# A two-layer FNet and MLP kernel: sums of the next tile, weights' steps and stores at other places in the order

## The chip, the cores and the metric

The kernel runs on one core of a Trainium2 chip. The metric is the device time of one execution in microseconds (us); three runs of the kernel before gave 2624.6, 2624.86 and 2625.03, a median of 2624.86 us. All times below are us unless ns is written. PE is the matrix engine (TensorE), PEld its weight loads, DVE the vector engine, ACT the scalar engine, POOL the GpSimd engine, and SP the queue that issues most transfers.

## The reference

```python
def _A_ref(x, dft_seq_re, dft_seq_im, dft_hid_re, dft_hid_im):
    a = jnp.einsum("bsd,ed->bse", x, dft_hid_re)
    b = jnp.einsum("bsd,ed->bse", x, dft_hid_im)
    y = jnp.einsum("ts,bse->bte", dft_seq_re, a) - jnp.einsum("ts,bse->bte", dft_seq_im, b)
    return y

def _B_ref(x, w1, b1, w2, b2):
    y = _layernorm(x, axis=-1)
    h = _gelu(jnp.einsum("bsd,df->bsf", y, w1) + b1)
    return jnp.einsum("bsf,fd->bsd", h, w2) + b2

x = A_x                                   # 1 x 2048 x 576, float32
x = x + _A_ref(_layernorm(x), ...)        # w1 is 576 x 4608, w2 is 4608 x 576
x = x + _B_ref(_layernorm(x), ...)
x = x + _A_ref(_layernorm(x), ...)
x = x + _B_ref(_layernorm(x), ...)
```

## The kernel before

All matrix products are made in a 2x2 block form with seven products in place of eight, and each float32 operand is cut into a high part (rounded to PE's float32r type by ACT, a "high") and a low part (source minus high, by DVE, a "low"). A product is then three passes: high by high, high by low, low by high (`PASSES`, L47).

**Sequence stage** (class `Sequence`, `run` at L758). The transform along the sequence comes first. Tiles 0 and 1 are made by `first_mms`; then 14 tiles (2 to 15) follow, each of seven products in the order 1, 6, 2, 5, 7, 3, 4 (`ORDER`, L34), each product 24 matmuls of 128x288. For a tile `cs` delivers four blocks of 128x1024 floats (0 to 3), loaded through SP into a ring of six buffers. A buffer that is given back is loaded at once with the next block in the order 0, 2, 3, 1 of the tiles (`load_c`, L677). The operands of products 5, 6, 2 and 7 are sums of blocks, made by DVE: `sums` (L688) makes block 2 + block 3 into a buffer `tmp` and subtracts block 0 from block 2; `low` (L700) goes on with the rest. Product n's low is recorded two products ahead, its high three ahead:

```python
                if n and n + 2 < len(steps):
                    self.low(*steps[n + 2])
                if n % 7 == 2 and t + 1 < NT:
                    self.sums(t + 1)
                self.load_c()
                if n + 3 < len(steps):
                    self.high(*steps[n + 3])
                self.mms(t, i)
```

The engines execute in the order that this code records. The third block of the next tile (block 3) can be loaded only when block 0 of this tile has been given back, which `low` of product 2 does (L705 to L707).

**Weights' steps** (generator `weights`, L264; `pump`, L322). While the first Sequence stage and the first MLP half run, w1 is cut into parts in DRAM, 126 parts in all: loads of 128x384 (`in_w`), GpSimd sums of them, two ACT operations (L284, L285), one DVE low (128x384, shown as 128x3x128) and a store to `w_parts` (L299). One `pump` does either the low of a part and the high of the next, or the store; the two alternate. In the Sequence stage each product but the third of a tile is followed by two pumps (L793 to L795), and there the stores are issued by ACT's queue. In the second layer no parts are left to make.

**MLP** (`mlp`, L1121; `inner`, `outer`). For one half of the rows, w1's products run in 18 steps q of seven products each (`inner`, 49 matmuls of 128x512), w2's in 9 groups g of two q each (`outer`, 128x288). q = 0 is made in two halves of 256 columns, the second inside group 0. Each product, and each half of an outer product, is followed by `advance` (L1195), which counts places: 0 to 6 for the first q of a group, 7 to 14 for the first outer products, 15 to 21 for the second q and so on (in group 0, which has no outer products, 0 to 6 and 7 to 13). At a place it pumps as often as `BEHIND` lists the place, in groups 1 and up; and in the first MLP it makes w2's parts (`make`, L1162): for each of seven products an ACT high (L1169), a DVE low (128x576), GpSimd differences, and a store. In this half the stores go through SP, as do w1's parts on their way back (`R<-w_parts`, by `load_w` at L1144). Group 0's w2 parts are made so: product 1 at places 3 and 4 of group 0; products 5, 6, 3, 7, 4 and 2 in group 1, from place 0 on (L1386 to L1392).

Of the kernel before, what the change touches and what calls it, by code (L numbers as in the profile page):

```python
# [15 lines left out]
P = 128  # L16
NT = S // P
DH = D // 2
NP = NT // 2
NQ = F // P // 2  # L20
NG = NQ // 2
# [40 lines left out]
EXTRA_AT = 7424  # L62
EARLY_X = (12800, 9344, 8192)
EARLY_T = 10496
BEHIND = (0, 2, 2, 4, 5, 6, 15, 16, 16, 17, 17, 19, 21, 21)
H_AT = (8704, 22400)
C2_AT = (OWN_AT, 37760)
Y_AT = (RN - Y_N, 0)
# [92 lines left out]
def spectral_mixer(ctx: ExitStack, tc: tile.TileContext, x, dh, c0, cs, w1, b1, w2, b2, out):  # L161
# [168 lines left out]
    class Sequence:  # L330
# [354 lines left out]
        def block(self, t, k):  # L685
            return self.live[t, k](NP, P)

        def sums(self, t):  # L688
            add(nc.vector, self.tmp(NP, P), self.block(t, 2), self.block(t, 3))
            sub(nc.vector, self.block(t, 2), self.block(t, 2), self.block(t, 0))  # L690

        def source(self, t, i):
            return self.tmp(NP, P) if i == 5 else self.block(t, {1: 0, 6: 0, 2: 1, 7: 2, 3: 1, 4: 3}[i])
# [64 lines left out]
        def run(self, hidden):  # L758
            for p in range(NP):
                while self.ready <= p:  # L760
                    next(self.pieces)
                self.first_mms(p)

            outs = [next(b for b in self.xs if b.at != raw.at)]
            self.xs.remove(outs[0])
            self.first_post(0, outs[0])
            for _ in self.pieces:
                pass
            outs.append(A.place(UV_AT + 4 * D, 2 * D) if outs[0].at < UV_AT + 4 * D else A.place(UV_AT + 6 * D, 2 * D))
            steps = self.steps  # L770
            for n, (t, i) in enumerate(steps):
                self.load_c()
                if n and n + 2 < len(steps):
                    self.low(*steps[n + 2])
                if n % 7 == 2 and t + 1 < NT:
                    self.sums(t + 1)
                self.load_c()
                if n + 3 < len(steps):
                    self.high(*steps[n + 3])
                self.mms(t, i)  # L780
                if n == 1:
                    self.first_turn(0, outs[0])
                    hidden.reserve()
                self.post(t, i)
                if n == 1:
                    self.first_post(1, outs[1])
                if n == 3:
                    self.first_turn(1, outs[1])
                if t == NT - 1:
                    hidden.begin(self, ORDER.index(i))  # L790
                if n == 3 and not self.early:
                    dma(b1t, b1)
                if n % 7 != 2 and n > 3 and (t < NT - 1 or n % 7 < 4):  # L793
                    pump()
                    pump()  # L795
            for k in range(2):
                self.L[k].free()
            self.own.close()
            for z in self.Z:
                z.free()  # L800
            hidden.take()
# [319 lines left out]
    def mlp(hid, store, first, ends, before, after):  # L1121
# [72 lines left out]

        def advance(to=None):  # L1195
            at[1] += to is None
            for _ in range(BEHIND.count(at[0]) if to is None and group[0] else 0):
                pump()
            while kept and kept[0][0] <= at[1]:
                kept.pop(0)[1]()  # L1200
            while due and due[0][0] <= (at[0] if to is None else to):
                due.pop(0)[1]()
            at[0] += 1
# [176 lines left out]
        for k in range(4 * first):  # L1380
            load_raw(0, k)
        for g in range(NG + 1):
            at[0], group[0] = 0, g or not first
            if first and not g:
                soon, late = make(0)
                due.extend((n, step) for n, (_, step) in zip((3, 4), soon))  # L1386
            elif first:
                due.extend(late)
                if g < NG:
                    soon, late = make(g)  # L1390
                    due.extend(soon)
            if g == NG:  # L1392
                work(99)
                hs.close()
            if half == 0 and len(c2.idle) < 4:
                more = R.place(0, 4 * DH)
                if more:
                    c2.idle.append(more)
            for f in range(2):
                if g < NG:  # L1400
                    for _ in inner(2 * g + f, None if g or f else 1):
                        pass
                if g == last and f:
                    c1.close()
                    Y.free()
                    if half == 0 or ends:
                        c2.idle += [R.place(C1_AT[half] + k * 4 * DH, 4 * DH) for k in range(2 + half)]
                    if half == 0:
                        c2.idle += [R.place(UT_AT[1][1] + k * 4 * DH, 4 * DH) for k in range(2)]
                if g == NG:  # L1410
                    if f == 0:
                        advance(6)
                        at[0], slot[0] = 7, 0
                        for k, i in enumerate(LAST):
                            outer(last, i, k % 2)
                elif g:
                    advance(6 + 15 * f)
                    at[0] = 7 + 15 * f
                    slot[0] = 0
                    for i in OUTER[f]:  # L1420
                        outer(g - 1, i, 1 - f)
# [87 lines left out]
```

## Time and profile before

| what | value |
|---|---|
| median of 3 runs | 2624.86 |
| the profiled execution | 2624.75 |
| its span, first to last instruction | 2623.0 |
| PE busy, PEld busy | 2614.4, 2466.3 |
| DVE, ACT, POOL busy | 1836.8, 1120.2, 791.5 |
| PE's granted clock over the span | 1.000 |
| chain that ended last: PE, DVE, transfers | 92%, 5%, 1% |

PE's matmuls are pipelined and their ends are modelled, so a PE that is busy all the time can still start its matmuls later than it could. A stretch that holds a known number of matmuls shows that by its length. The first Sequence stage runs to about 376 us, the first MLP half from about 438 to 870.

### The profile page before, as it was taken

Reading aid. Unit: us, or ns where it says so; the run is one execution under the profiler, and the core shown is the slowest. Engines: PE = TensorE matmul, PEld = TensorE weight load, DVE = VectorE, ACT = ScalarE, POOL = GpSimd, SP = SyncE. Lnnn points to the kernel's source line nnn. Section 1 sums busy time; section 2 is a strip of 40 time slices with the busy share of each in tenths; the row PEclk is TensorE's granted clock in tenths of the full one; section 3 lists DMA queues with packets and bytes.
Section 4 is the critical chain, followed back from the end, with each engine's and each line's share of the span. In section 5 each row is a group of like instructions: output and inputs, shape, how many; then the busy total and the mean of one; then the engine's idle time right before and its main releaser. Section 6 shows DMA issues by size and latency. Waiting matters only on the chain.

```text
span 2623.0 us, 44794 instructions
## 1 busy us (share of the span) xinstructions
PE 2614.4 (100%) x17252; PEld 2466.3 (94%) x17252; DVE 1836.8 (70%) x2580; ACT 1120.2 (43%) x1821; POOL 791.5 (30%) x638
## 2 busy tenths in 40 slices
PE   9999999999999999999999999999999999999999
PEld 9999999899999989998999999999999999899998
DVE  8999987778787765556687776576555557655555
ACT  7555555555553443333354333353333325433332
POOL 5334333544444332222251000132122233322222
PEclk9999999999999999999999999999999999999999
DMA  6667676778788666676544343756666685666664
GB/s 226 223 236 234 234 255 215 266 278 301 279 299 300 178 202 195 194 222 210 173 175 135 122 124 124 211 159 194 193 195 194 195 268 169 199 195 195 194 194 155
DMA packets 223238, 544.91 MB, mean 208 GB/s; under 512 B 23712, under 2 KB 74912, under 8 KB 222880
## 3 DMA queue, kind: packets, MB, share of 16 engines
q1 hardware_dynamic: 210496, 513.91, 62.2%
q10 hardware_dynamic: 12528, 28.12, 2.8%
q8 instruction: 137, 2.24, 0.3%
q14 instruction: 77, 0.63, 0.1%
HBM read 429.87 MB, written 114.72 MB: 208 GB/s over the span
## 4 chain that ended last, share of the span: by engine, by line
PE 92%; DVE 5%; DMA 1%; issue 1%; POOL 1%; ACT 0%; DVEq 0%; ACTq 0%; SPq 0%; POOLq 0%
PE bank L211 91%; DVE R L201 3%; DVE A L201 1%; DMA w_parts<-R 1%; DMA A<-in_cs 0%; PE bank L991 0%; DVE A L198 0%; PE bank L1035 0%; DVE moments L242 0%; PE bank L994 0%; ACT R L698 0%; DMA A<-in_w 0%; DMA R<-w_parts 0%; PE bank L1045 0%; POOL A L198 0%
## 5 line engine op out<-in xcount | busy, mean ns | idle before, releaser
L211 PE MATMUL bank<-R 128*128 128x288 f32 (+2 forms) x16972 | 2585.9, 314 | 3.9 <-DVE R L201 1.2
L211 PEld LDWEIGHTS bank<-R 128*128 128x128 f32 x16972 | 2434.8, 189 | 150.8 <-DVE R L201 4.3
L198 DVE TENSOR_TENSOR A<-bank,A 128x576 f32<-128x576 f32 (+3 forms) x812 | 567.6, 707 | 510.2 <-PE bank L211 457.7
L201 POOL TENSOR_TENSOR R<-A,R 128x512 fp32r<-128x512 f32 (+1 forms) x292 | 380.0, 1310 | 912.4 <-ACT R L1299 560.6
L201 DVE TENSOR_TENSOR R<-A,R 128x1024 fp32r<-128x1024 f32 (+10 forms) x534 | 535.0, 1028 | 34.6 <-ACT R L698 14.3
L1299 ACT ACTIVATE R<-A 128x512 fp32r<-128x512 f32 x288 | 177.5, 630 | 356.4 <-DVE A L201 219.5
L198 POOL TENSOR_TENSOR A<-A 128x576 f32<-128x576 f32 (+2 forms) x102 | 155.0, 1527 | 531.1 <-ACT A L743 338.9
L1234 ACT ACTIVATE bank<-bank,b1t 128x512 f32<-128x512 f32 (+1 forms) x224 | 144.9, 647 | 350.5 <-DVE bank L198 233.6
L698 ACT ACTIVATE R<-A 128x1024 fp32r<-128x1024 f32 x196 | 205.6, 1054 | 123.8 <-PE bank L211 61.0
L198 DVE TENSOR_TENSOR bank<-bank,A 128x512 f32<-128x512 f32 (+1 forms) x228 | 152.3, 670 | 147.7 <-PE bank L211 147.0
L201 POOL TENSOR_TENSOR A<-A 128x288 f32<-128x288 f32 (+3 forms) x152 | 190.3, 1255 | 198.1 <-DVE R L201 103.6
L201 DVE TENSOR_TENSOR A<-A 128x1024 f32<-128x1024 f32 (+3 forms) x166 | 163.5, 989 | 6.2
L201 DVE TENSOR_TENSOR R<-bank,R 128x512 fp32r<-128x512 f32 x232 | 156.1, 676 | 5.5 <-ACT R L1299 5.0
L1299 ACT ACTIVATE R<-bank 128x512 fp32r<-128x512 f32 x216 | 121.0, 595 | 33.9 <-PE bank L211 33.9
L201 DVE TENSOR_TENSOR A<-bank,A 128x512 f32<-128x512 f32 x144 | 98.1, 681 | 0.4
L1261 ACT ACTIVATE A<-bank 128x512 f32<-128x512 f32 (+1 forms) x76 | 43.7, 575 | 120.2 <-PE bank L211 120.1
L284 ACT ACTIVATE R<-A 128x256 fp32r<-128x256 f32 x126 | 51.9, 412 | 63.7 <-DMA w_parts<-R 27.1
L1234 ACT ACTIVATE A<-bank,b1t 128x512 f32<-128x512 f32 (+1 forms) x76 | 50.5, 665 | 63.4 <-DVE bank L198 63.4
L232 POOL TENSOR_TENSOR moments<-moments,power 128x1 f32<-128x1 f32 x32 | 25.5, 797 | 134.9 <-DVE moments L234 117.5
L285 ACT ACTIVATE R<-A,power,middle 128x128 fp32r<-128x128 f32 x126 | 60.6, 481 | 0.0
L258 ACT ACTIVATE A<-A,moments 128x576 f32<-128x576 f32 x58 | 49.3, 867 | 23.7 <-DMA A<-x_mid 11.7
L198 DVE TENSOR_TENSOR A<-A 128x1024 f32<-128x1024 f32 x28 | 35.8, 1277 | 20.0 <-DMA A<-in_cs 12.3
(70 smaller groups left out, 612.9 us busy)
## 6 DMA issues: line engine op xcount, KB each, us to landing
R<-w_parts SPq DMA_DIRECT2D x504, 320.0 KB, 3.4
R<-w_parts SPq DMA_DIRECT2D x189, 576.0 KB, 3.7
A<-in_cs SPq DMA_DIRECT2D x112, 512.0 KB, 4.5
w_parts<-R SPq DMA_DIRECT2D x63, 576.0 KB, 6.2
w_parts<-R ACTq DMA_DIRECT2D x75, 320.0 KB, 4.3
w_parts<-R SPq DMA_DIRECT2D x51, 320.0 KB, 4.9
uv_mid<-A SPq DMA_DIRECT2D x28, 576.0 KB, 5.4
A<-in_w SPq DMA_DIRECT2D x72, 192.0 KB, 5.4
```

What stands on the lines that cost most here:

```text
L198: engine.tensor_tensor(dst, a, b, op=op)
L201: engine.tensor_tensor(dst, a, b, op=OP.subtract)
L211: nc.tensor.matmul(o, a, b, start=start, stop=stop, skip_group_check=True)
L232: nc.gpsimd.tensor_tensor(mv[:, 3:4], mv[:, 2:3], power[:, 0:1], op=OP.pow)
L258: nc.scalar.activation(dst, src, AF.Identity, bias=mv[:, 4:5], scale=mv[:, 3:4])
L284: nc.scalar.activation(t[:, 1:4:2], src[:, 0:3:2], AF.Copy)
L285: nc.scalar.activation(t[:, 2], src[:, 1], AF.Identity, bias=power[:, 2:3], scale=middle)
L698: nc.scalar.activation(self.cells[t, i](2, NP, P)[:, 0], self.source(t, i), AF.Copy)
L1234: nc.scalar.activation(dst, src, AF.Gelu_apprx_tanh, bias=bias(f))
L1261: nc.scalar.activation(up, o, AF.Copy)
L1299: nc.scalar.activation(H[q, k](2, TC)[:, 0], src, AF.Copy)
```

## The change

Five things are moved; no arithmetic is added or taken away.

1. `sums` of the next tile is cut in two: the addition behind the low that is recorded with product 4 of the tile (`n % 7 == 3`), the subtraction with product 5 (`n % 7 == 4`). Before, both stood with the third product.
2. The weights' steps in the Sequence stage are left out behind the seventh product of a tile and no longer behind the third; in the last tile they follow the first five products and no longer the first, second and fourth; in the first tile two products instead of three.
3. `BEHIND` has the same 14 pumps at other places, so that every store stands at a later place than its low.
4. In the second group of the first MLP half a shorter list, `BEHIND_1`, has 12 pumps.
5. w2's parts of products 5 and 6 for group 0 are made at places 5, 6, 12 and 13 of group 0, not at places 0 to 3 of group 1.

```diff
-BEHIND = (0, 2, 2, 4, 5, 6, 15, 16, 16, 17, 17, 19, 21, 21)
+BEHIND = (0, 2, 4, 4, 6, 6, 15, 16, 17, 17, 19, 19, 21, 21)
+BEHIND_1 = (0, 2, 4, 4, 15, 16, 17, 17, 19, 19, 21, 21)
...
-        def sums(self, t):
-            add(nc.vector, self.tmp(NP, P), self.block(t, 2), self.block(t, 3))
-            sub(nc.vector, self.block(t, 2), self.block(t, 2), self.block(t, 0))
+        def sums(self, t, which=(0, 1)):
+            if 0 in which:
+                add(nc.vector, self.tmp(NP, P), self.block(t, 2), self.block(t, 3))
+            if 1 in which:
+                sub(nc.vector, self.block(t, 2), self.block(t, 2), self.block(t, 0))
...
-                if n % 7 == 2 and t + 1 < NT:
-                    self.sums(t + 1)
+                if n % 7 in (3, 4) and t + 1 < NT:
+                    self.sums(t + 1, (n % 7 - 3,))
...
-                if n % 7 != 2 and n > 3 and (t < NT - 1 or n % 7 < 4):
+                if n % 7 != 6 and n > 3 and (t < NT - 1 or n % 7 < 5):
                     pump()
                     pump()
...
-            for _ in range(BEHIND.count(at[0]) if to is None and group[0] else 0):
+            for _ in range((BEHIND if group[0] > 1 else BEHIND_1).count(at[0]) if to is None and group[0] else 0):
                 pump()
...
-            at[0], group[0] = 0, g or not first
+            at[0], group[0] = 0, g if first else NG
             if first and not g:
                 soon, late = make(0)
-                due.extend((n, step) for n, (_, step) in zip((3, 4), soon))
+                due.extend((n, step) for n, (_, step) in zip((3, 4, 5, 6, 12, 13), soon + late[:4]))
+                late = late[4:]
```

The built programs show where the instructions went. Lines of the change are numbered one to four higher.

**DVE, one tile of the first Sequence stage, before.** The stretch begins with the row that reads block 0 for the last time (after it block 3 of the next tile can be loaded). `R<-A,R 128x1024` is a low of a product, `128x3x128` a weights' step, `A<-bank` the reading of product 6's sum; the two `A<-A 128x1024` in the middle are the next tile's sums.

```order
L201 TENSOR_TENSOR A<-A 128x1024
L201 TENSOR_TENSOR R<-A,R 128x3x128
L201 TENSOR_TENSOR R<-A,R 128x1024
L198 TENSOR_TENSOR A<-bank,A 128x288
L201 TENSOR_TENSOR R<-A,R 128x3x128
L201 TENSOR_TENSOR R<-A,R 128x1024
L198 TENSOR_TENSOR A<-A 128x1024
L201 TENSOR_TENSOR A<-A 128x1024
L201 TENSOR_TENSOR R<-A,R 128x1024
L201 TENSOR_TENSOR R<-A,R 128x3x128
L201 TENSOR_TENSOR R<-A,R 128x1024
```

The same stretch of the change, from the same row.

```order
L202 TENSOR_TENSOR A<-A 128x1024
L202 TENSOR_TENSOR R<-A,R 128x3x128
L202 TENSOR_TENSOR R<-A,R 128x1024
L199 TENSOR_TENSOR A<-bank,A 128x288
L202 TENSOR_TENSOR R<-A,R 128x3x128
L202 TENSOR_TENSOR R<-A,R 128x1024
L202 TENSOR_TENSOR R<-A,R 128x3x128
L202 TENSOR_TENSOR R<-A,R 128x1024
L199 TENSOR_TENSOR A<-A 128x1024
L202 TENSOR_TENSOR R<-A,R 128x3x128
L202 TENSOR_TENSOR R<-A,R 128x1024
L202 TENSOR_TENSOR A<-A 128x1024
```

The addition (L199) now has a weights' step and a low more between itself and the first row, the subtraction a further two.

**ACT, group 0 of the first MLP half, before.** `R<-A 128x2x288` is the high of a w2 part, `bank<-bank,b1t` and `A<-bank,b1t` are gelus, `A<-bank 128x512` is the copy of product 1's sum of q = 1.

```order
L1169 ACTIVATE R<-A 128x2x288
L1234 ACTIVATE bank<-bank,b1t 128x256
L1234 ACTIVATE A<-bank,b1t 128x256
L1234 ACTIVATE bank<-bank,b1t 128x512
L1299 ACTIVATE R<-bank 128x512
L1261 ACTIVATE A<-bank 128x512
```

The same stretch of the change.

```order
L1172 ACTIVATE R<-A 128x2x288
L1237 ACTIVATE bank<-bank,b1t 128x256
L1172 ACTIVATE R<-A 128x2x288
L1237 ACTIVATE A<-bank,b1t 128x256
L1237 ACTIVATE bank<-bank,b1t 128x512
L1302 ACTIVATE R<-bank 128x512
L1264 ACTIVATE A<-bank 128x512
```

The high of w2's part 5 stands ahead of two gelus and of the copy.

**SP, the second q of group 1, before.** `R<-w_parts 128x640` loads a part of w1, `L299` stores one.

```order
L299 DMA w_parts<-R 128x640
L195 DMA R<-w_parts 128x640
L299 DMA w_parts<-R 128x640
L195 DMA A<-in_w 128x384
L195 DMA R<-w_parts 128x640
```

The same stretch of the change.

```order
L300 DMA w_parts<-R 128x640
L196 DMA R<-w_parts 128x640 x2
L300 DMA w_parts<-R 128x640
L196 DMA A<-in_w 128x384
L196 DMA R<-w_parts 128x640
```

The second load no longer stands behind the second store.

## Rows read from the trace of the kernel before

**Rows 1.** Windows, tiles 5 to 8, 10 and 12 to 15 of the first Sequence; columns in its head line.
```profile
core 0: us, PE busy (x) PEld busy (x) DVE busy (x) ACT busy (x) POOL busy (x), PEclk, DMA share, GB/s
...
126.87:149.27 22.40, 22.40 (x170) 22.28 (x169) 20.89 (x22) 12.69 (x23) 7.63 (x5) 1.00 0.69 240
149.27:172.67 23.40, 22.81 (x170) 22.35 (x169) 21.75 (x22) 12.88 (x23) 6.58 (x5) 1.00 0.66 229
172.67:195.68 23.01, 22.93 (x171) 22.41 (x170) 22.05 (x24) 13.35 (x24) 6.78 (x5) 1.00 0.68 228
195.68:219.07 23.39, 22.73 (x171) 22.35 (x169) 20.49 (x22) 12.80 (x24) 8.02 (x6) 1.00 0.68 232
...
241.34:263.56 22.22, 22.22 (x171) 22.22 (x169) 21.71 (x21) 12.59 (x24) 10.22 (x6) 1.00 0.74 244
...
285.77:308.44 22.67, 22.52 (x171) 22.28 (x169) 21.41 (x22) 12.66 (x23) 7.44 (x5) 1.00 0.68 239
308.44:331.34 22.90, 22.76 (x170) 22.31 (x169) 21.75 (x24) 13.04 (x24) 7.03 (x5) 1.00 0.67 235
331.34:353.91 22.57, 22.52 (x170) 22.28 (x169) 21.68 (x22) 12.49 (x23) 9.18 (x7) 1.00 0.65 222
353.91:376.12 22.21, 22.21 (x170) 22.21 (x169) 18.92 (x24) 16.80 (x29) 6.69 (x5) 1.00 0.80 266
```
**Rows 2.** Groups by form, DVE, 126.87 to 353.91 (tiles 5 to 14): busy, mean ns, idle before.
```profile
L201 DVE TENSOR_TENSOR R<-A,R 128x1024 fp32r<-128x1024 f32 x70 | 98.9, 1413 | 2.7 <-ACT R L698 2.7
L201 DVE TENSOR_TENSOR R<-A,R 128x384 fp32r<-128x384 f32 x60 | 45.0, 750 | 0.0
...
L198 DVE TENSOR_TENSOR A<-A 128x1024 f32<-128x1024 f32 x10 | 13.0, 1304 | 7.9 <-DVE R L201 3.7 <-issue 3.2 <-DMA A<-in_cs 1.0
```
**Rows 3.** Timeline of SP, tile 8: start, duration.
```profile
203.12 0.33 SPq L195 DMA_DIRECT2D A<-in_cs  x1
```
**Rows 4.** Timeline of DVE, tile 8: start, duration, in brackets the idle time before.
```profile
209.18 1.23 DVE L198 TENSOR_TENSOR A<-A 128x1024 f32<-128x1024 f32 x1 [2.08 <-issue]
```
**Rows 5.** Timeline of DVE, lows of product 6 in tiles 10 and 11.
```profile
241.90 1.23 DVE L201 TENSOR_TENSOR R<-A,R 128x1024 fp32r<-128x1024 f32 x1 [0.29 <-ACT R L698]
...
264.41 1.23 DVE L201 TENSOR_TENSOR R<-A,R 128x1024 fp32r<-128x1024 f32 x1 [0.29 <-ACT R L698]
```
**Rows 6.** Groups by form, POOL, 126.87 to 353.91.
```profile
L201 POOL TENSOR_TENSOR A<-A 128x384 f32<-128x384 f32 x25 | 40.0, 1601 | 28.0 <-issue 20.2 <-DMA w_parts<-R 5.8 <-DVE R L201 1.1
```
**Rows 7.** Windows, groups 0 and 1 of the first MLP half.
```profile
452.02:469.77 17.75, 17.75 (x79) 14.53 (x78) 11.14 (x19) 11.46 (x22) 7.67 (x6) 1.00 0.83 271
469.77:501.68 31.91, 30.00 (x168) 25.76 (x166) 26.33 (x39) 17.84 (x36) 17.71 (x14) 1.00 0.68 233
```
**Rows 8.** Timeline of PEld, 440 to 506.
```profile
471.69 1.48 PEld L211 LDWEIGHTS bank<-R 128*128 128x128 f32 x7 [0.57 <-DVE A L198]
474.16 5.54 PEld L211 LDWEIGHTS bank<-R 128*128 128x128 f32 x36 [0.99 <-DVE bank L198]
480.74 18.41 PEld L211 LDWEIGHTS bank<-R 128*128 128x128 f32 x109 [1.04 <-POOL R L201]
499.95 6.20 PEld L211 LDWEIGHTS bank<-R 128*128 128x128 f32 x41 [0.80 <-DVE R L201]
```
**Rows 9.** Timeline of DVE, group 1, low of w2's part 6.
```profile
471.55 0.74 DVE L201 TENSOR_TENSOR R<-A,R 128x576 fp32r<-128x576 f32 x1
```
**Rows 10.** Timeline of SP, second q of group 1.
```profile
495.38 0.32 SPq L299 DMA_DIRECT2D w_parts<-R  x1
```
**Rows 11.** Chain of waits, 440 to 506: start, duration, what.
```profile
496.28 3.57 DMA R<-w_parts
```
**Rows 12.** Timeline of POOL, group 0, both differences for w2's part 1.
```profile
451.76 2.93 POOL L201 TENSOR_TENSOR A<-A 128x576 f32<-128x576 f32 x2 [3.74 <-DVE R L201]
```
**Rows 13.** Timeline of ACT, group 0.
```profile
452.01 0.48 ACT L1234 ACTIVATE A<-bank,b1t 128x256 f32<-128x256 f32 x1 [0.49 <-DVE bank L198]
...
453.84 0.60 ACT L1261 ACTIVATE A<-bank 128x512 f32<-128x512 f32 x1
```
**Rows 14.** Windows, second layer's Sequence.
```profile
1400.00:1500.00 100.00, 100.00 (x759) 100.00 (x758) 69.96 (x68) 39.52 (x51) 9.50 (x10) 1.00 0.41 133
```

## The prediction

> **What bounds the kernel now.** I read the windows view by tile first, then the groups of one engine, then its timeline. PE is busy throughout, but its ends are modelled, so I compare the length of a stretch with the matmuls in it. A Sequence tile is seven products of 24 matmuls. Tile 10 takes 22.22 and tile 15 takes 22.21 [rows 1], that is 22.21 / 168 = 0.1322 a matmul, with weight loads without a gap. I take that as the floor. Above it lie tile 5 by 0.19, tile 6 by 1.19, tile 7 by 0.80, tile 8 by 1.18, tile 12 by 0.46, tile 13 by 0.69 and tile 14 by 0.36 [rows 1]: 4.87 us in all. That is everything the Sequence part of the change can win. In the second layer 759 matmuls in 100 us are again 0.1318 each, with no gap in the weight loads, so nothing is to be had there [rows 14].
>
> What makes these tiles late is DVE. It is busy 20.5 to 22.1 in each, of 22.21 that PE needs [rows 1]. Among its groups only the first of the next tile's sums waits noticeably: 7.9 us before ten of them [rows 2], in part under the name of a transfer, in part as "issue" or as DVE itself. The timeline shows what it is: block 3 of the next tile is issued at 203.12 [rows 3], and the addition starts at 209.18 after 2.08 of waiting [rows 4], 6.06 after the issue. The lows behind it in DVE's order wait too, and PE waits for them.
>
> The second place is the start of the MLP. From 452.02 to 469.77 PE makes 11 products of 7 matmuls (the count of 79 takes in both neighbours), 17.75 / 77 = 0.2305 each [rows 7]. The next stretch, to 501.68, holds ten more such products and 96 outer matmuls: 70 x 0.2305 + 96 x 0.1322 = 28.8, but takes 31.91 [rows 7], 3.1 too long. The weight loads stand still four times there: 0.57 and 0.99 behind DVE, 1.04 behind POOL and 0.80 before 499.95 [rows 8], in all 3.40. Before the last one a load of w1's parts issued at 496.28 lands after 3.57 [rows 11], so that one is a transfer's, though the row names DVE.
>
> **The sums.** Between the last reading of block 0 and the addition stood two weights' steps and two lows, 2 x 0.75 + 2 x 1.41 = 4.3. Now there are three of each, 6.5 [rows 2], against the 6.06 that the load took in the longest wait [rows 3, 4]. I take the waits as gone. DVE then has, in the seven late tiles, a mean of 21.4 us of work (the mean of their DVE column [rows 1]) and room of 0.8 a tile. Nothing else moves against PE: counted from one low of product 6 to the next, DVE does the same work. The lows of products 2, 5 and 7 come a weights' step earlier, those of 3 and 4 by two sums and one sum, those of 1 and 6 unchanged.
>
> Not every tile has room. From the low of product 6 in tile 10 to that in tile 11 are 264.41 - 241.90 = 22.51, without a wait for the load [rows 5], 0.30 more than PE needs. It is covered by a lead: that low ends at 243.13, and product 6 is due at 241.34 + 22.21 / 7 = 244.51, so 1.38 ahead [rows 1, 5]. Tiles with and without room alternate in runs of three or four, because the weights come in sevens and a tile holds six steps; three such tiles use 0.9 of the lead. I leave 0.4 us for what remains and take **4.5 saved**, of bounds 0 and 4.87.
>
> **The weights' steps in the Sequence.** They are as many, but one fewer in tile 2 and two more in tile 15. Tile 15 has DVE busy 18.92 of 22.21 [rows 1]; two steps of 0.75 fit. If that cover were gone (the first hidden products wait for a cut that stands behind them), the cost is at most these 1.5. Taken as 0. The second layer's Sequence has no weights' steps and DVE at 70 of 100 [rows 14]: 0.
>
> **w2's parts 5 and 6 in group 0.** From the stretch 466 to 475 two lows of 0.74 [rows 9], two highs on ACT and one weights' step of 0.75 on DVE [rows 2] go away: 2.2 us of DVE, against stalls of 0.57 + 0.99 behind it [rows 8]. POOL loses one difference of 1.47, half of 2.93 [rows 12], in front of the lows that PE waits 1.04 for [rows 8]. So the first three stalls should go.
>
> What is new stands in group 0. The high of part 5 reads the difference that POOL makes at 451.76, the first of two in 2.93 [rows 12], so it can start only at 453.2. It lasts about 0.7 (the low of that tile takes 0.74 [rows 9]) and stands on ACT ahead of the gelu that started at 452.01 and of the copy at 453.84 [rows 13]. Gelu to copy took 1.83, so the copy starts at 453.2 + 0.7 + 1.83 = 455.8 at the latest and ends at 456.4. The third product of q = 1 writes the bank that is copied and is due at 452.02 + 14 x 0.2305 = 455.25. **A new stall of 0.7 to 1.1; I take 0.95.** Part 6, two places before the end of group 0, has free time on all engines: 0.
>
> **The stores one place later.** In the second q of group 1 the store at 495.38 [rows 10] stands behind a low of its own place, and the load PE waits for can be issued only behind it, at 496.28 [rows 11]. With the load ahead of the store, it can go when its buffer comes free, some 3 us sooner: the last stall, 0.80 by the weight loads, goes. In the other groups of this half I see no stall to win. Together the MLP gives 3.1 - 0.95 = **2.1 saved**, of bounds 2.7 (3.40 - 0.7) and a loss of 1.1 (all stalls stay).
>
> **Sum.** 2624.75 - 4.5 - 2.1 = 2618.15 for the profiled execution. The median of the runs lies 0.11 above it, so 2618.3.
>
> **The rivals.** Two tenths of a per cent, 5.25 us, is about what a measurement of this kernel can tell from no change; below 2619.6 it is faster.
>
> *Contention fills the gap.* DVE's steps are stretched where POOL works: the 1024-wide low takes 1.41 in the mean and 1.23 by itself [rows 2, 5]. If every tile comes to need the 22.51 of tile 10, thirteen tiles lose 0.30 each less the lead of 1.38, so 2.5: only 2.4 are won, 2620.4. For it: waiting tiles have less DVE work than tile 10, as if the wait kept the engines apart. Against it: tile 10 has also the most POOL work, 10.22, and that is given by the weights' order [rows 1].
>
> *A full stop at each meeting.* If DVE, at one more meeting per tile, had to wait out a POOL sum whole, 1.60 [rows 6], the room of 0.8 would leave 0.8 lost in each of thirteen tiles, 10.4 in place of 4.87; with 2.1 won, 2628.3. Against it: 25 such sums last 40.0 in tiles 5 to 14 [rows 6], yet all 70 lows together are stretched by only 70 x 0.18 = 12.6 [rows 2, 5]. The Trainium skill (SBUF — State Buffer, section Who interferes with whom) does say that a DVE instruction with two SBUF inputs and a GpSimd one that reads SBUF exclude each other for a whole instruction; this trace agrees that they hinder each other and not that it is for so long.
>
> *The MLP gives nothing.* The stall behind the new high remains and the others shrink by no more than it costs, because they have a second cause behind the first (the four lows on POOL follow each other with or without the difference). 2624.86 - 4.5 = 2620.4.
>
> *Slower: the load comes later too.* Block 3 is issued through SP in order, behind loads of weights that wait for POOL to free their buffer. If it came so late that the addition still waits 1.5 a tile, DVE would need 21.4 + 0.4 + 1.5 = 23.3, and thirteen tiles would lose 1.1 each, 14: with 4.87 no longer lost and 2.1 won, 2632. It decides from a wait of about 0.8 a tile upward, today's mean. Against it: the change takes away the pumps just ahead of that load, and the largest delay seen is 6.06.
>
> **How the numbers follow.** The forecast has 0.60, contention 0.16, the full stop 0.02, the MLP without gain 0.14, the late load 0.05, no effect at all 0.03. The forecast's own range is 2617.0 to 2620.0 (all of 4.87 and 2.5, or 3.5 and 1.3). The range of 2616.9 to 2622.5 adds both rivals at 2620.4, with 2 us for both at once. Five in six of the forecast and a third of the first two rivals lie below 2619.6: faster 0.61. Above 2630.1 lie the late load and a little of the unknown: slower 0.06. The rest, 0.33, is the same.
>
> **What would show it.** Tiles 5 to 14 at 22.2 to 22.3 each, and no idle time on DVE before its first sums. If the waits are gone and tiles are still long, contention was right; if the addition still waits, the late load. In the MLP: one gap of about 1 us in the weight loads near 455 (moved by what the Sequence saves), with ACT's part-5 high waiting for POOL ahead of it; none of the four later ones. A gap of 2 us there, or the POOL stall still present, would make the MLP's term wrong.

## The result and the profile after

The change is slower, by a quarter of a per cent: a median of 2631.52 us over ten runs (2628.47 to 2635.53) against 2624.89 for ten runs of the kernel before (2623.43 to 2625.95), a ratio of 1.0026 with an interval of 1.0016 to 1.0035. The prediction was 2618.3, in a range that ended at 2622.5. The profiled execution of the change has a span of 2629.1, that of before 2623.0.

To split the 6.1 us I use one mark that every trace has: the short run of weight loads with which the transpositions ahead of the first MLP half end. In the timeline of PEld, before:

```profile
442.61 0.85 PEld L1035 LDWEIGHTS bank<-ident,A 128*128 128x128 f32 x8 [0.17 <-DVE A L201]
```

The same timeline after the change, 440 to 770 (start, duration, line, tiles, count, and in brackets the idle time before with what ended it):

```profile
442.14 0.85 PEld L1038 LDWEIGHTS bank<-ident,A 128*128 128x128 f32 x8 [0.17 <-DVE A L202]
455.41 11.14 PEld L212 LDWEIGHTS bank<-R 128*128 128x128 f32 x49 [0.90 <-ACT A L1264]
468.56 38.65 PEld L212 LDWEIGHTS bank<-R 128*128 128x128 f32 x228 [2.01 <-ACT A L1264]
508.12 45.18 PEld L212 LDWEIGHTS bank<-R 128*128 128x128 f32 x266 [0.91 <-ACT R L1302]
554.61 45.01 PEld L212 LDWEIGHTS bank<-R 128*128 128x128 f32 x266 [1.31 <-ACT R L1302]
600.73 45.02 PEld L212 LDWEIGHTS bank<-R 128*128 128x128 f32 x266 [1.11 <-ACT R L1302]
647.01 44.93 PEld L212 LDWEIGHTS bank<-R 128*128 128x128 f32 x266 [1.27 <-ACT R L1302]
692.78 44.91 PEld L212 LDWEIGHTS bank<-R 128*128 128x128 f32 x266 [0.84 <-ACT R L1302]
738.40 31.69 PEld L212 LDWEIGHTS bank<-R 128*128 128x128 f32 x189 [0.70 <-ACT R L1302]
```

Up to the mark the change wins 0.5 us where 4.5 were forecast; behind it, it loses 6.6 where 2.1 were to be won. The four gaps of [rows 8] are gone. In their place stand two in group 0, of 0.90 and 2.01, and one at the start of every later stretch of outer products, six of them here, 6.14 in all. New less old is 6.14 + 2.91 - 3.40 = 5.65; the other 0.9 lies in pieces too small to name.

**The gap that comes back in every group** is read from the chain of waits of the change, 500 to 560 (start, duration, what):

```profile
498.90 5.17 DMA w_parts<-R
...
543.98 6.58 DMA w_parts<-R
...
550.64 0.18 ACT R L285
...
551.99 1.00 ACT R L1302 x2
...
554.64 5.50 PE bank L212 x33
```

and from ACT's timeline, in group 0 (first two rows) and later:

```profile
452.76 0.69 ACT L1172 ACTIVATE R<-A 128x576 fp32r<-128x576 f32 x1 [1.71 <-POOL A L202]
...
467.91 0.60 ACT L1264 ACTIVATE A<-bank 128x512 f32<-128x512 f32 x1 [4.16 <-POOL R L202]
...
550.64 0.42 ACT L285 ACTIVATE R<-A 128x256 fp32r<-128x256 f32 x1 [3.65 <-DMA w_parts<-R]
```

A store of a part of w1 is issued at 543.98 and lands 6.58 later. ACT stands still for 3.65 until then, in the high of a later part (L285), and behind that high in ACT's order stand the last gelu and the H highs (L1302) that the outer products read. The highs write into a ring of three buffers (`stage(3, 5 * P)[:, n % 3]`), so the high of part n + 1 has to wait for the store of part n - 2. Of the lows of a group at places 17, 19 and 21, the first had its store at place 17 before and has it at 19 now; the high that needs that buffer follows the low of place 21. The distance fell from four places to two. Places 15 to 21 are products of the second q, seven matmuls each, 7 x 0.2305 = 1.6 us [rows 7]: the distance went from 6.4 to 3.2, against landings of 5.17 and 6.58.

**The gap of 2.01** has its cause on POOL, whose timeline reads in group 0:

```profile
465.23 1.43 POOL L202 TENSOR_TENSOR A<-A 128x576 f32<-128x576 f32 x1 [2.80 <-DVE R L202]
466.62 1.26 POOL L202 TENSOR_TENSOR R<-A,R 128x512 fp32r<-128x512 f32 x1
```

The first row is the difference for w2's part 6, the second the last of the four H lows of q = 0. The difference itself waits 2.80 for DVE's low of part 6, and the H low, recorded behind it, waits with it. The copy at 467.91 takes over the buffer which that H low reads, and it is PE that waits for the copy.

**The Sequence**, tiles 6, 7 and 12 of the change, by windows (columns as in [rows 1]):

```profile
150.21:172.73 22.52, 22.48 (x170) 22.25 (x169) 20.54 (x22) 12.43 (x23) 8.60 (x6) 1.00 0.66 242
172.73:196.13 23.40, 22.85 (x171) 22.38 (x170) 21.53 (x24) 13.35 (x24) 7.45 (x5) 1.00 0.65 233
...
284.98:308.21 23.23, 22.77 (x170) 22.30 (x169) 21.25 (x22) 12.53 (x23) 6.59 (x5) 1.00 0.63 227
```

Against a floor of 22.21, tiles 8 and 14 lose nothing any more and tile 6 only 0.31, where it lost 1.19 [rows 1]; but tile 7 now loses 1.19 and tile 12 loses 1.02. The groups by form of the change say what waits, from 126.59 to 353.9 in the first three rows, from 500 to 760 in the last:

```profile
L202 DVE TENSOR_TENSOR R<-A,R 128x384 fp32r<-128x384 f32 x61 | 42.4, 695 | 9.0 <-ACT R L286 7.6 <-DMA w_parts<-R 1.4
L199 DVE TENSOR_TENSOR A<-A 128x1024 f32<-128x1024 f32 x10 | 13.0, 1300 | 1.1 <-issue 1.1
L285 ACT ACTIVATE R<-A 128x256 fp32r<-128x256 f32 x61 | 25.3, 415 | 69.0 <-DMA w_parts<-R 43.4 <-DVE R L202 13.1 <-POOL A L199 10.9
...
L285 ACT ACTIVATE R<-A 128x256 fp32r<-128x256 f32 x39 | 16.1, 412 | 36.4 <-DMA w_parts<-R 36.4
```

The same ACT group before, in the same two stretches:

```profile
L284 ACT ACTIVATE R<-A 128x256 fp32r<-128x256 f32 x60 | 24.8, 414 | 51.2 <-DMA w_parts<-R 21.4 <-DVE R L201 17.8 <-POOL A L198 11.0
...
L284 ACT ACTIVATE R<-A 128x256 fp32r<-128x256 f32 x39 | 15.9, 408 | 0.7 <-DMA w_parts<-R 0.5
```

The addition's wait fell from 7.9 [rows 2] to 1.1, as forecast. But DVE now waits 9.0 in front of the weights' lows, where it had waited 0.0 [rows 2]: for ACT's highs, and these wait twice as long for stores (43.4 against 21.4). In the MLP the same wait rose from 0.5 to 36.4.

What reaches PE is seen in the waits of the weight loads from 82 to 376 (total, times, longest), the change first, then before:

```profile
PEld bank L212 <- ACT A L746: 1.6, 3, 0.7
PEld bank L212 <- ACT A L744: 1.2, 4, 0.4
PEld bank L212 <- DVE R L202: 0.3, 1, 0.3
...
PEld bank L211 <- DVE R L201: 3.3, 8, 0.9
```

The waits for DVE's lows went, as forecast, from 3.3 to 0.3. In their place PE waits 2.8 for ACT (0.4 before), which copies the sums of products 5 and 7 out of their banks (L744, L746). In ACT's order these copies stand behind the weights' highs, as here ahead of a gap of 0.69 in tile 7:

```profile
190.75 0.42 ACT L285 ACTIVATE R<-A 128x256 fp32r<-128x256 f32 x1 [1.88 <-DMA w_parts<-R]
...
192.41 0.39 ACT L746 ACTIVATE A<-bank 128x288 f32<-128x288 f32 x1
```

So both stages lose by the same cause: a high waits on ACT for the store that frees its buffer, and something that PE needs stands behind it.

### The profile page after: what moved, and what is told of

Same layout as the page of the kernel before. It is cut to its first block, busy times and chain, and to the rows that moved or that the text cites. A ratio compares the mean times of both kernels' runs of the same rounds, so it can differ in the third digit from the quotient of the medians.

```text
span 2629.1 us, 44796 instructions
## 1 busy us (share of the span) xinstructions
PE 2615.9 (99%) x17252; PEld 2466.9 (94%) x17252; DVE 1831.3 (70%) x2580; ACT 1117.1 (42%) x1821; POOL 786.9 (30%) x638
## 4 chain that ended last, share of the span: by engine, by line
PE 80%; DMA 2%; ACT 1%; DVE 1%; issue 0%; POOL 0%; DVEq 0%; ACTq 0%
PE bank L212 79%; DMA w_parts<-R 1%; ACT R L1302 1%; PE bank L994 0%; PE bank L1038 0%; DVE R L202 0%; DMA R<-w_parts 0%; PE bank L997 0%; ACT bank L1237 0%; DVE A L199 0%; ACT R L1172 0%; PE bank L1048 0%; ACT R L286 0%; DVE A L202 0%; DVE bank L199 0%
## 5 line engine op out<-in xcount | busy, mean ns | idle before, releaser
L199 DVE TENSOR_TENSOR A<-bank,A 128x576 f32<-128x576 f32 (+3 forms) x812 | 568.2, 707 | 508.0 <-PE bank L212 446.5
L1302 ACT ACTIVATE R<-A 128x512 fp32r<-128x512 f32 x288 | 177.7, 630 | 343.6 <-DVE A L202 218.7
L199 POOL TENSOR_TENSOR A<-A 128x576 f32<-128x576 f32 (+2 forms) x102 | 150.6, 1483 | 543.0 <-ACT A L746 340.6
L199 DVE TENSOR_TENSOR bank<-bank,A 128x512 f32<-128x512 f32 (+1 forms) x228 | 152.3, 670 | 146.2 <-PE bank L212 145.4
L1302 ACT ACTIVATE R<-bank 128x512 fp32r<-128x512 f32 x216 | 120.6, 595 | 28.7 <-PE bank L212 28.7
L285 ACT ACTIVATE R<-A 128x256 fp32r<-128x256 f32 x126 | 52.1, 414 | 127.0 <-DMA w_parts<-R 92.8
L259 ACT ACTIVATE A<-A,moments 128x576 f32<-128x576 f32 x58 | 49.3, 867 | 23.9 <-DMA A<-x_mid 11.9
L202 DVE TENSOR_TENSOR A<-A,bank 128x512 f32<-128x512 f32 x72 | 48.8, 678 | 0.0
```

The source lines that it names most:

```text
L199: engine.tensor_tensor(dst, a, b, op=op)
L202: engine.tensor_tensor(dst, a, b, op=OP.subtract)
L259: nc.scalar.activation(dst, src, AF.Identity, bias=mv[:, 4:5], scale=mv[:, 3:4])
L285: nc.scalar.activation(t[:, 1:4:2], src[:, 0:3:2], AF.Copy)
L1302: nc.scalar.activation(H[q, k](2, TC)[:, 0], src, AF.Copy)
```

## The experiments

"Mark" is the start of the row named above, "behind" the span less the mark. The ratio is to runs of before on the same chip, whose medians were 2624.59 to 2624.89.

| kernel | median | ratio, interval | span | mark | behind |
|---|---|---|---|---|---|
| before | 2624.89 | 1 | 2623.0 | 442.61 | 2180.4 |
| the change | 2631.52 | 1.0026, 1.0016 to 1.0035 | 2629.1 | 442.14 | 2187.0 |
| e1, change with the old places | 2624.15 | 1.0000, 0.9990 to 1.0009 | 2623.0 | 441.44 | 2181.6 |
| e2, new places alone | 2633.55 | 1.0038, 1.0025 to 1.0051 | 2630.3 | 441.25 | 2189.1 |
| e3, Sequence part alone | 2622.34 | 0.9992, 0.9982 to 1.0001 | 2619.6 | 439.88 | 2179.7 |
| e4, w2's parts alone | 2625.92 | 1.0006, 0.9997 to 1.0016 | 2624.5 | 442.58 | 2181.9 |
| e5, sums alone | 2621.90 | 0.9989, 0.9980 to 0.9998 | 2619.8 | 438.54 | 2181.3 |
| e6, pause alone | 2621.85 | 0.9990, 0.9980 to 0.9999 | 2620.3 | 440.73 | 2179.6 |
| e7, change, last low later | 2627.48 | 1.0014, 1.0004 to 1.0023 | 2625.3 | 440.58 | 2184.7 |
| e8, mended | 2621.84 | 0.9988, 0.9979 to 0.9998 | 2619.9 | 441.32 | 2178.6 |
| e9, mended, old pause | 2617.91 | 0.9974, 0.9963 to 0.9984 | 2616.2 | 438.15 | 2178.1 |
| e10, the same, a tile later | 2618.07 | 0.9975, 0.9965 to 0.9985 | 2617.2 | 438.45 | 2178.8 |
| e11, change, part 6 later | 2630.11 | 1.0021, 1.0011 to 1.0031 | 2630.5 | 440.27 | 2190.2 |

Span and mark are those of one execution each. Up to the mark, before, e2 and e4 run the same code, and their marks differ by 1.4; those of the six kernels with the Sequence code of the change differ by 2.3. One difference of marks of that size shows nothing; groups of kernels that lie apart do.

### The stores: e1, e2 and e7

e1, against the change:

```diff
-BEHIND = (0, 2, 4, 4, 6, 6, 15, 16, 17, 17, 19, 19, 21, 21)
+BEHIND = (0, 2, 2, 4, 5, 6, 15, 16, 16, 17, 17, 19, 21, 21)
```

> The changed kernel with the old list of places from group 2 on (group 1 keeps the new short list). Theory A (a store one place later means that the scalar engine, two weights' steps on, waits for that store's landing before it may write the same one of three buffers, and holds the copies behind it that the matrix engine needs): the stalls of 1.3, 1.1, 1.2, 0.8 and 0.7 us at the first outer products of groups 2 to 6 go, about 5 of the 6 us, and the span comes near 2624. Rival B (moving w2's parts 5 and 6 forward shifts everything that follows, and the stalls come from that): they stay, span near 2629. In both the stalls of 0.9 and 2.0 in group 0 and the first of group 1 stay.

Timeline of PEld in e1:

```profile
467.85 38.59 PEld L212 LDWEIGHTS bank<-R 128*128 128x128 f32 x228 [2.01 <-ACT A L1264]
507.37 262.80 PEld L212 LDWEIGHTS bank<-R 128*128 128x128 f32 x1548 [0.93 <-ACT R L1302]
```

Of the six gaps only the first is left. It comes from group 1, whose own shorter list has the same last places as the change's. From there 1548 weight loads run without a gap, and the span is 2623.0, as expected of the first theory.

e2 is the reverse edit, the new `BEHIND` put into the kernel before.

> The kernel before with the new list of places alone, in all groups. Theory A: the stalls of about 1 us per group appear here too, in groups 2 to 6 and perhaps in group 1, while the late load at 499 in group 1 goes (-0.6): span 2623.0 + 5 to 6, near 2628.5. Rival B: no stall in groups 2 to 6, span near 2622.5.

Timeline of PEld in e2; the second row is the first of eight gaps from 500 on:

```profile
479.83 26.59 PEld L211 LDWEIGHTS bank<-R 128*128 128x128 f32 x164 [1.05 <-POOL R L201]
507.30 44.92 PEld L211 LDWEIGHTS bank<-R 128*128 128x128 f32 x266 [0.88 <-ACT R L1299]
```

One line of numbers brings the gaps and makes the kernel before slower by 0.38% (five runs). The span is 1.8 above what was expected: besides six gaps behind ACT there are two behind DVE, of 0.43 and 1.22, which were not followed. The gap at 499.95 of [rows 8] is gone too, as the prediction said it would be with the load no longer behind the store.

e7 keeps every store of the change where it is and moves one low, against the change:

```diff
-BEHIND = (0, 2, 4, 4, 6, 6, 15, 16, 17, 17, 19, 19, 21, 21)
+BEHIND = (0, 2, 4, 4, 6, 6, 15, 16, 17, 17, 19, 19, 21, 23)
```

> The changed kernel, all its stores where it has them, only the last low of a group two places later (and with it the high that takes the buffer of the store two parts earlier). If that high, which waits on ACT for the landing of a store issued two places ahead of it, makes the stalls of groups 2 to 6, they go (5.9 us in all, to under 1.5) and the span falls from 2629.1 to 2623 to 2625. If a store or a low at a later place costs by itself (DVE and SP beside the H products), they stay and the span is 2628 or more.

PEld's timeline in e7, then, in the second fence, its ACT group from 500 to 760:

```profile
506.29 20.88 PEld L212 LDWEIGHTS bank<-R 128*128 128x128 f32 x121 [0.83 <-ACT R L1302]
...
552.00 44.95 PEld L212 LDWEIGHTS bank<-R 128*128 128x128 f32 x266 [0.30 <-issue]
```

```profile
L285 ACT ACTIVATE R<-A 128x256 fp32r<-128x256 f32 x39 | 16.1, 412 | 25.1 <-DMA w_parts<-R 24.1 <-DVE R L202 1.0
```

ACT still waits 24.1 for stores, but the H highs now stand ahead of that wait, and five gaps of 0.70 to 1.31 become 0.30. The first, of the shorter list, stays at 0.83. The stretch behind the mark is 2.3 shorter, not the 4.4 or more expected: the six gaps sum to 2.33 in place of 6.14, but two of 0.39 and 0.69 opened at DVE. So it is not a later store by itself that makes the six gaps, but what is queued on ACT behind a high whose buffer has not been stored. A ring of four buffers, the other remedy, was not tried.

### The w2 parts: e4, e8 and e11

e4, against before:

```diff
-                due.extend((n, step) for n, (_, step) in zip((3, 4), soon))
+                due.extend((n, step) for n, (_, step) in zip((3, 4, 5, 6, 12, 13), soon + late[:4]))
+                late = late[4:]
```

> The kernel before with w2's parts 5 and 6 moved into group 0 alone. The stall of 0.9 us behind the high of part 5 appears near 455, and one of 2.0 near 467, where GpSimd's difference for part 6 stands ahead of the last low of q = 0, whose source is a buffer that the next q waits for; the three stalls at 471, 474 and 480 (2.3 us) go, the late load at 499 (0.7) stays. Span 2623.0 + 2.9 - 2.3, near 2623.6. Rival: the buffer has another cause (the scalar engine), and the stall at 467 is missing: span near 2621.6.

PEld's timeline in e4:

```profile
455.83 11.14 PEld L211 LDWEIGHTS bank<-R 128*128 128x128 f32 x49 [0.89 <-ACT A L1261]
468.97 12.09 PEld L211 LDWEIGHTS bank<-R 128*128 128x128 f32 x64 [2.00 <-ACT A L1261]
482.07 18.42 PEld L211 LDWEIGHTS bank<-R 128*128 128x128 f32 x109 [1.01 <-POOL R L201]
501.54 268.52 PEld L211 LDWEIGHTS bank<-R 128*128 128x128 f32 x1593 [1.05 <-DVE R L201]
```

By the gaps this part costs more than it wins: 0.89 + 2.00 come, 0.57 and 0.99 go, and POOL's gap, which was expected to go too, stays. By its ten runs it can't be told from before (0.9997 to 1.0016).

e11, against the change, moves one step:

```diff
-                due.extend((n, step) for n, (_, step) in zip((3, 4, 5, 6, 12, 13), soon + late[:4]))
-                late = late[4:]
+                due.extend((n, step) for n, (_, step) in zip((3, 4, 5, 6, 12), soon + late[:3]))
+                late = [(0, late[3][1])] + late[4:]
```

> The changed kernel with one step moved: the low of w2's part 6, and with it POOL's difference for that part, behind the last place of group 0 in place of place 13. If that difference, ahead of the last H low on POOL, makes the stall of 1.7 near 467, that one goes and the stall of 0.6 near 454 (part 5, not moved) stays; the stalls of groups 2 to 6 stay, and the span is 2627 to 2628. If the stall near 467 has another cause, it stays at 1.7.

PEld's timeline in e11:

```profile
453.54 49.88 PEld L212 LDWEIGHTS bank<-R 128*128 128x128 f32 x277 [0.89 <-ACT A L1264]
504.88 44.91 PEld L212 LDWEIGHTS bank<-R 128*128 128x128 f32 x266 [1.47 <-ACT R L1302]
```

The gap of 2.01 is gone, and that of 0.89 stays as it was, so the two have the two causes named. The span was not 2627 to 2628: the gaps of the later groups came out at 0.86 to 2.23 in this execution, 9.1 in all against 6.1. The chain holds six stores in both executions; their times to landing add up to 35.7 in the change and 37.7 here. As many stores are waited for, and how late they land differs.

e8 leaves out the new places, keeps the Sequence part, and puts both parts of w2 where nothing that PE waits for stands behind them. Against before, beside the Sequence part:

```diff
-                due.extend((n, step) for n, (_, step) in zip((3, 4), soon))
+                due.extend((n, step) for n, (_, step) in zip((3, 4, 8, 9, 12), soon + late[:3]))
+                late = [(0, late[3][1])] + late[4:]
```

> The kernel before with the Sequence part of the change, the stores of groups 2 to 6 as before, and in group 0 the high of w2's part 5 behind the last gelu and copies that PE waits for (place 8 in place of 5) and the low and difference of part 6 behind the last of the H lows. If the two stalls that the change brings to group 0 (0.6 near 455 and 1.7 near 467) come from POOL's difference standing ahead of what PE waits for, both are gone, of the 1.5 us that the Sequence part alone loses from 466 to 482 under 0.8 is left, and the span is 2618.3 to 2619.3. If they come from the mere number of steps in group 0, stalls of 1 us or more show elsewhere before 470 and the span is 2620 or more.

PEld's timeline in e8:

```profile
465.74 51.28 PEld L211 LDWEIGHTS bank<-R 128*128 128x128 f32 x294 [0.62 <-ACT R L1301]
```

The two new gaps and the four old ones are gone; in their place is one of 0.62, and the stretch behind the mark is 1.1 shorter than in e3. The span, 2619.9, lies 0.6 above the expected range: the mark came 1.4 later than in e3, with the same Sequence code.

### The Sequence: e3, e5 and e6

e3 is parts 1 and 2 of the change, alone.

> The kernel before with the Sequence part alone (sums split, no weights' step behind the seventh product). The Sequence tiles of the first layer together lose 3.7 us above 22.21 each, as in the changed kernel, against 4.9 before; a wait of the vector engine for the scalar engine's weights' high takes the place of its wait for the block. The MLP keeps its four stalls of 3.1. Span about 2622. Rival (the Sequence part is worth what was predicted, and its loss came through parts made earlier or later): tiles lose under 1 us, span about 2618.5.

Groups by form in e3, 126.87 to 353.91:

```profile
L201 DVE TENSOR_TENSOR R<-A,R 128x384 fp32r<-128x384 f32 x61 | 42.7, 700 | 6.2 <-ACT R L285 6.1
L284 ACT ACTIVATE R<-A 128x256 fp32r<-128x256 f32 x61 | 25.3, 415 | 67.3 <-DMA w_parts<-R 39.8 <-DVE R L201 13.1 <-POOL A L198 10.9
```

Without the rest of the change the new wait on ACT is there as well. The span of 2619.6 lies between the two expectations, and the MLP did not keep its four stalls: POOL's is 0.53 in place of 1.04, and the last one, at 499.95 before, is missing though the stores are at their old places. e5 and e6 take the two halves apart. e5 has the sums of the change and the old rule of the pumps:

```diff
...
-                if n % 7 == 2 and t + 1 < NT:
-                    self.sums(t + 1)
+                if n % 7 in (3, 4) and t + 1 < NT:
+                    self.sums(t + 1, (n % 7 - 3,))
```

> The kernel before with the two sums behind products 4 and 5, the weights' steps and the MLP as before. Both halves together gave a span of 2619.6 against 2623.0, with 1.9 us lost in the late tiles of the Sequence against 4.9. If it is the later addition that does it (the load of block 3 has more time before DVE asks for it), this run gives it alone: a span of 2619 to 2620.5, and no DVE wait of 2 us for in_cs. If it is the weights' step left out ahead of that load, this run stays at 2622 to 2623.5 and the late tiles lose 4 to 5 us.

e6 has the old sums and the new rule:

```diff
-                if n % 7 != 2 and n > 3 and (t < NT - 1 or n % 7 < 4):
+                if n % 7 != 6 and n > 3 and (t < NT - 1 or n % 7 < 5):
```

> The kernel before with no weights' step behind the seventh product (and one behind the third), the sums and the MLP as before. If the later addition brings the gain, this run stays within 1 us of a span of 2623.0, DVE still waits some 8 us before the additions. If the weights' step in front of the load brings it, the span is 2619 to 2620.5 and these waits are down to 2 us in all.

Windows of e5 (tile 3, and tiles 4 to 14), and its ACT group in the same stretch as above:

```profile
82.27:105.49 23.22, 22.52 (x171) 22.29 (x169) 22.29 (x22) 13.01 (x24) 10.20 (x6) 1.00 0.62 211
105.49:349.83 244.34, 244.34 (x1850) 244.34 (x1849) 225.48 (x234) 144.44 (x257) 93.63 (x60) 1.00 0.70 241
```

```profile
L284 ACT ACTIVATE R<-A 128x256 fp32r<-128x256 f32 x62 | 25.7, 415 | 42.6 <-DMA w_parts<-R 23.9 <-DVE R L201 7.9 <-POOL A L198 6.4
```

In e6 the addition waits as before:

```profile
L198 DVE TENSOR_TENSOR A<-A 128x1024 f32<-128x1024 f32 x10 | 13.1, 1306 | 8.1 <-DVE R L201 3.5 <-issue 3.4 <-DMA A<-in_cs 1.2
```

e5 came out as the later addition would have it: eleven tiles in 244.34, that is 22.21 each, the floor, and 1.0 lost once, in tile 3. ACT's wait for stores is 23.9 there, 39.8 with the new pause. e6 fits neither expectation: the addition waits as long as ever, and the span is still 2.7 shorter. Of this 0.8 lies behind the mark, where POOL's stall is halved and the last stall missing, as in e3; what it wins ahead of the mark (1.9 against before, 0.5 against e2) stays open.

The two halves together win no more than either alone: the medians of e3, e5 and e6 lie within 0.5. So the later sums fill the tiles, and with them in place the pause behind the seventh product costs. All kernels bear this out: the three with the later sums and the old pause (e5, and e9 and e10 below, which have it from tile 3 or 4 on) have their marks at 438.15 to 438.54, the six with the later sums and the new pause (the change, e1, e3, e7, e8, e11) at 439.88 to 442.14. The landing of the stores, which ACT's queue issues here, differs in the same way. From 126.87 to 353.91 (count, KB each, median us to landing), the change first, then e5:

```profile
w_parts<-R ACTq DMA_DIRECT2D x61, 320.0 KB, 5.1
...
w_parts<-R ACTq DMA_DIRECT2D x63, 320.0 KB, 3.4
```

This median is 4.8 to 5.3 in those six kernels, 3.3 to 3.6 in the three, and 3.7 to 4.1 in before, e2, e4 and e6. So ACT waits longer at least in part because the same stores land later; why they do is not shown.

### Put together: e9 and e10

e9 is e8 with the pause behind the third product again from tile 3 on (`PLAIN` is 2); e10, with `PLAIN + 1` in the same place, from tile 4 on. e9 against e8:

```diff
-                if n % 7 != 6 and n > 3 and (t < NT - 1 or n % 7 < 5):
+                if n % 7 != (2 if PLAIN < t < NT - 1 else 6) and n > 3 and (t < NT - 1 or n % 7 < 5):
```

> The mended kernel of the run before, with the weights' steps of tiles 3 to 14 again left out behind the third product, as in the kernel before, and behind the seventh in tile 2 alone; the sums stay behind products 4 and 5. If the pause in the weights' steps has to stand ahead of the sums (the sums alone, with that pause, lost 0.7 us from 100 to 440 where both halves together lose 2.6 to 4.4), the late tiles again lose under 1.2 us, the stall at 92 is gone with one step less ahead of it, and the span is 2616 to 2617.5. If the low loss of the sums alone was the chance of one execution, the tiles lose 2.5 or more and the span is 2619 or more.

> The same, with the pause behind the seventh product in tiles 2 and 3 and behind the third from tile 4 on. If the stall at 92 in the run with the sums alone comes from too many weights' steps in tile 2, this run is like the last one, 2616 to 2617.5. If it comes from the pumps behind products 4 to 6 of tile 2 and 1 and 2 of tile 3 as such, that one keeps the stall of 1 us and this one loses it, being shorter by 1.

e9 by windows (tiles 4 to 14 without the ends), and its chain of waits from 440 to 870 by line:

```profile
105.00:349.00 244.00, 244.00 (x1848) 244.00 (x1847) 223.02 (x234) 144.84 (x257) 90.85 (x59) 1.00 0.70 242
```

```profile
by line: PE bank L211 99.4%; PE bank L993 0.2%; PE bank L1047 0.2%; ACT R L1301 0.1%; PE bank L996 0.1%; issue 0.0%
```

The first row is 0.1320 a matmul without a gap, and in the second PE alone sets the end. e9 beats both kernels, 4.5 ahead of the mark and 2.3 behind it: the two terms that were forecast, by other edits. It differs from e8 in the pause alone, and its slowest run (2619.15) is faster than e8's fastest (2620.40). e10 agrees within what can be measured. The stall in tile 3 is gone in both, as expected if it came of the weights' steps behind the last product of tile 2.

## Why the prediction was wrong, by its own steps

**The sums** (4.5 forecast). The mechanism was right and its size too: DVE's wait fell from 7.9 to 1.1, and with the sums alone the mark comes 4.07 earlier, in e9 4.46. In the change itself it was 0.5 in the profiled execution; the mark lies 1.2 to 2.7 ahead of before in the five other kernels with the same Sequence code.

**The weights' steps in the Sequence** ("Taken as 0") is the first step that failed. I counted them and asked whether DVE had room, and did not follow the three steps that each part passes through: its high needs a buffer that a store gives back. With the later sums and the pause behind the seventh product, ACT's highs wait 40 to 44 us for stores in place of 21 (before) or 24 (e5), the copies behind them come late for PE, and of the 4.5 us that e9 wins ahead of the mark 1.7 to 4.0 are lost again. e5 against e3, and e9 against e8, show that it is the pause, and e6, with 29.9, that the pause alone does less; that it works by putting the two sums into the middle of the run of six pumped products, in place of its start, is argued from the order alone.

**w2's part 5**: 0.95 forecast, 0.90 found, and its high on ACT waits 1.71 for POOL ahead of the gap, as was to be seen if the step was right.

**w2's part 6** ("free time on all engines: 0") failed. POOL was free, but what it had to do next was awaited: with a difference of 1.43, and its wait of 2.80 for DVE, put in front of the last H low, the weight loads stood still for 2.01. The working had priced the same difference when it was taken away in group 1, and not where it went.

**The three stalls that go.** The first two went, by the cause given. The third, POOL's 1.04, did not go by w2's parts (1.01 in e4); it halves with the Sequence part (0.53 in e3, which has one weights' step more done by then) and is gone only with both (e8). **The last stall** went as forecast, in e2 by the places alone. But it is missing in e3, e6 and e8 too, which have the old places: the Sequence part alone takes it away, which the prediction did not see.

**"In the other groups of this half I see no stall to win"** is the step that turned the sign. It was true, and it was all that was said of these groups: that a moved store could lose something there was given no bound. The trace before held it. ACT waits 0.5 in 39 highs there, with a median landing of 5.0 inside a distance of 6.4; a look at who next writes the buffer that the store frees, and at the distance left, would have shown that 3.2 is too little. Six groups made 6.14 of it, and with the old places in groups 2 and up (e1) the median is 2624.15 again.

**The rivals.** None was it. The late load gave 2632, near the result, by a mechanism that did not occur: the addition waits 1.1 in ten tiles, so the nearness is chance. Contention and the full stop fall with e5: once the waits are gone, eleven tiles in a row take 22.21. The MLP did not give nothing, it took. Two small sums were off as well: with 4.87 and 2.5 won the forecast's own range would begin at 2617.5, and the parts of "faster" add up to 0.60; neither matters here.

On the landing time the Trainium skill has a rule (DMA: Bandwidth & Descriptors, section Anatomy of one DMA — SWDGE (gpsimd) path): a fixed 2.0 us and the bytes at 436 GB/s, for transfers issued by GpSimd. For these 320 KB, issued by SP, that would be an estimate of 2.75 us, less than two places, and no gap. The trace differs: 6.58 in the chain above. The four such stores of 540 to 556 land after a median of 5.5, at a time when the DMA engines, in 40 slices of the stretch in tenths, are busy nearly throughout. No run here shows such a store by itself, so whether the load makes the difference stays open.

```profile
DMA  5886988999999999999999999999999999999998
```

## What to carry to other kernels

When a step is put later, ask which buffer it gives back, who writes that buffer next, and what stands behind that writer on its engine; the slack is the distance in time between the two, to be set against the landing time of the trace. An engine that is free at a place has no room there if the next thing it does is awaited: an added step holds that up by its own length and by whatever the step itself waits for. What two edits win alone need not add up, so run each half alone, and the whole mended by what they show.

## What the runs showed of the hardware

The time of a store from issue to landing is not a constant that one can schedule against to the microsecond. In the Sequence the same 320 KB stores land after medians of 3.3 to 5.3 us, in thirteen kernels that do the same work in another order; in the chain of the change in the MLP they land after 5.17 to 6.58. Between two executions the same six gaps added up to 6.1 and 9.1. The runs of the change lie within 7.1 us and those of e9, whose chain holds no landing from 440 to 870, within 1.9; but e4, without such a store in its chain, spreads by 6.3, and e7, with two, by 2.9, so that the landings make the spread is not shown.

The same DVE step does not always take the same time: the weights' low took 750 ns before [rows 2], 695 in the change, 700 in e3 and 620 in e5, with no edit to it. What stretches it was not traced.
